# Windowed attention and a low-rank mixer on one core: head-pair scores on two 64-row halves, and batch 1's attention placed inside the first MLP chunk

## Chip, cores and metric

One core of a Trainium2 chip (trn2). The metric is the device time of one execution in microseconds (us), lower is better; 0.3% (1.2 us) is about what a measurement of this kernel can tell from no change.

## What is computed

Eight batches, eight heads, 576 positions, head size 64. Causal attention in a window of 64 positions, then, per batch, a mixer of rank 32 along the sequence and a two-layer MLP (512 to 2048 to 512), both with a residual:

```python
scores = scale * np.matmul(q, k.transpose(0, 1, 3, 2))
rel = pos[:, None] - pos[None, :]
scores = np.where((rel >= 0) & (rel < 64), scores, -1000000000.0)
attn = softmax(scores)
x = (attn @ v) with the heads side by side          # B, S, 512
u = x + ((x.transpose(0, 2, 1) @ U) @ V).transpose(0, 2, 1)
out = u + np.maximum(u @ w_ch1, 0.0) @ w_ch2
```

## The kernel before

All matmuls are in bf16. A batch has 576 = 9 blocks of 64 positions; a block of queries sees two blocks of keys. A tile named `un` holds 128 tokens of `u`, and the MLP works on nine chunks of 512 tokens across the batches, so chunk 0 needs batch 0 alone, chunk 1 batches 0 and 1, and so on.

**Attention of one batch** (`attention`) is a table of pieces. T: `TK`, `TQ` transpose keys and queries of a head pair on TensorE (L249 for batches 0 to 3, 12 transposes of 96 rows to 64 columns; L255 for the others) and copy them out of PSUM. Keys go by ScalarE into `kt` (L267). Queries go into a block-diagonal `qbd`, in which the other head's half is zero: one half by ScalarE (L276), the other by VectorE (L278), which waits for the first. S: `SC`, two per pair, computes the scores with 9 full matmuls per pair (L292, 128 keys by 128 columns, both heads at once), the exponential on ScalarE (L300), the mask on VectorE (L302). PV: five pieces of up to 16 matmuls (L320) that write the halves of PSUM's partitions by turns, then on VectorE a reciprocal (L329) and the normalisation into `xs` (L330). U, V: the mixer (L344, cast L352, L359) and on VectorE the sum with `xs` into `un` (L368). UT: transposes of `un` (L381) and copies into `uTc` (L385), which the MLP reads. Values of even blocks are needed shifted by 64 partitions: `shift_v` (L132 to 141) copies `vA` to `vB`.

**MLP of one chunk** (`mlp`) is 32 slots of four 512-column matmuls: slots 0 to 15 are the first layer (L407), evicted with relu by VectorE (odd, L416) and ScalarE (even, L418); slots 16 to 31 the second (L429), and after every fourth the residual sum into `osb` on VectorE (L438).

**Order.** The engines execute their instructions as the program writes them. Batch 0's attention comes first, alone. Then chunk 0's 32 slots, with nothing between, then batch 1's attention alone, with its value shifts on VectorE ahead of each PV. From chunk 1 on, `PLACE` says after which slot of chunk c a piece of batch c+1 is written (and T of batch c+2):

```python
PLACE = {"S": [0, 2, 4, 6, 8, 10, 12, 14], "PV": [16, 17, 18, 19, 20],
         "T": [16, 17, 18, 19, 20, 21, 22, 23], "U": [22], "V": [24, 25, 26],
         "UT": [26, 27, 28, 29, 30]}
```

Batch 2's T and S stand in chunk 1 too, from slot 4 (T) and 7 (S). PSUM: `ps_mm` has three one-bank buffers (MLP; three of four transposes of batches 0 and 1), `ps_big` two two-bank buffers (scores, PV, mixer), `ps_tp` one bank (all other transposes). Loads stand on GpSimd's queue.

Of the kernel before, what the change touches and what calls it, by code (L numbers as in the profile page):

```python
# [17 lines left out]
def kernel(  # L18
# [41 lines left out]
    pt_pool = ctx.enter_context(tc.tile_pool(name="pt", bufs=1))  # L60
# [13 lines left out]
    maskA = const.tile([P, 5, 2, W], BF16, name="maskA")  # L74
# [12 lines left out]
    qbd = [const.tile([P, 2, S], BF16, name=f"qbd{j}") for j in range(HP)]  # L87
# [75 lines left out]
    for i in range(2):  # L163
# [3 lines left out]
        out=maskA[:, 0, :, :],  # L167
        in_=maskA[:, 0, :, :],
# [7 lines left out]
        out=maskA[:, 1:5, :, :],  # L176
        in_=maskA[:, 1:5, :, :],
# [3 lines left out]
        pattern=[[0, 4], [0, 2], [-1, W]],  # L181
# [3 lines left out]
        out=maskA[:, 1:5, :, :],  # L185
        in_=maskA[:, 1:5, :, :],
# [3 lines left out]
        pattern=[[0, 4], [0, 2], [1, W]],  # L190
# [36 lines left out]
    def attention(b, spare=False):  # L227
# [6 lines left out]
        pts = [None] * HP  # L234
# [35 lines left out]
        def TQ(j):  # L270
            def f():
                tp = tr(qb, j)
                for g in range(2):
                    rs = slice(g * W, g * W + W)
                    if g == 0:
                        nc.scalar.copy(out=like(qbd[j][rs, g, :]), in_=tp[rs])  # L276
                    else:
                        nc.vector.tensor_copy(out=like(qbd[j][rs, g, :]), in_=tp[rs])  # L278
            return f

        def SC(j, part):
            blks = range(0, 5) if part == 0 else range(5, NB)
            n = len(blks)

            def f():
                if part == 0:
                    pts[j] = pt_pool.tile([P, NB, 2, W], BF16, name=f"pt{j}")
                pt = pts[j]
                sc = ps_big.tile([P, 2 * CH], FP32, name="sc", tag="big")
                for kk, blk in enumerate(blks):  # L290
                    w0 = 0 if blk == 0 else W * (blk - 1)
                    nc.tensor.matmul(  # L292
                        sc[:, kk * P : (kk + 1) * P],
                        kt[j][:, w0 : w0 + P],
                        qbd[j][:, :, blk * W : (blk + 1) * W],
                        start=True,
                        stop=True,
                    )
# [4 lines left out]
            return f

        def PV(t):
            def f():
# [4 lines left out]
                for h in range(H):  # L311
                    for blk in blks:
# [5 lines left out]
                        else:  # L318
# [3 lines left out]
                            pts[h // 2][:, blk, h % 2, :],  # L322
# [66 lines left out]
        pcs["S"] = [SC(j, a) for j in range(HP) for a in range(2)]  # L389
# [9 lines left out]
    def mlp(c):  # L399
# [68 lines left out]
    def values_and_mixing(b, a):
        for t in range(NT):
            if t < NFULL:  # L470
                shift_v(b, nc.vector, [t])
            a["PV"][t]()
        for part in ("U", "V", "UT"):
            for f in a[part]:
                f()


    att = {0: attention(0, True)}
    transposes_and_scores(att[0])
# [8 lines left out]
    for c in range(NCH):  # L488
        slots = [[] for _ in range(NSLOT)]

        def place(b, part):
            for f, s in zip(att[b][part], PLACE[part]):
                slots[s].append(f)

        if c == 0:
            att[1] = attention(1, True)
            for f in mlp(0):
                f()
            transposes_and_scores(att[1])
            for _ in load_kq(3, False):  # L500
                pass
            values_and_mixing(1, att[1])
            continue
        b = c + 1
        if b < B:
            shift_v(b, nc.gpsimd)
            if b + 1 < B:
                load_v(b + 1)
            if b + 2 < B:
                for _ in load_kq(b + 2, False):  # L510
                    pass
            if b == 2:
                att[2] = attention(2)
                for n, f in enumerate(att[2]["T"]):
                    slots[FIRST_T + n].append(f)
                for n, f in enumerate(att[2]["S"]):
                    slots[FIRST_T + 3 + n].append(f)
            else:
                place(b, "S")
            place(b, "PV")  # L520
            if b + 1 < B:
                att[b + 1] = attention(b + 1)
                place(b + 1, "T")
            for part in ("U", "V", "UT"):
                place(b, part)
        for fill, extra in zip(mlp(c), slots):
            fill()
            for f in extra:
                f()
# [30 lines left out]
```

## Time and profile before

| | |
|---|---|
| three runs | 389.4, 389.86, 390.8 us; median 389.86 |
| profiled execution | 390.55 us, of it 388.5 from first to last instruction |
| TensorE busy | 343.6 us (88%), 2739 matmuls |
| VectorE, ScalarE, GpSimd busy | 189.9, 144.7, 104.6 us |
| mean granted TensorE clock | 0.969 |
| chain that ended last | TensorE 78%, VectorE 9%, ScalarE 4%, GpSimd 3% |

Busy time overlaps between engines. The chain runs back from the last instruction, at each step to what released it. TensorE's matmuls are pipelined, so the distance of two starts tells the pace, not the length of a row. A granted clock of 1.0 is 2.4 GHz, 0.5 is 1.2 GHz; before its first recorded change it reads 1.0 whatever it was.

### The profile page before, as it was taken

The numbers are of one execution on the slowest core, as the hardware profiler recorded it, in microseconds if no ns is written. First come the engines' busy times: TensorE is split into PE (matmuls) and PEld (weight loads), VectorE is DVE, ScalarE is ACT, GpSimd is POOL, SyncE is SP. The second block draws the span as 40 slices with busy tenths as digits, with TensorE's granted clock in tenths as the row PEclk, the third lists the DMA queues.
The fourth block names the chain that finished last, engine by engine and source line by source line (L and its number), as shares of the span: only waits on it lengthen the run. The fifth ranks groups of instructions, "written<-read, shape, count | busy, mean of one in ns | idle before, by whom it ended". The sixth has DMA issues, their size and how long they took to land.

```text
span 388.5 us, 6618 instructions
## 1 busy us (share of the span) xinstructions
PE 343.6 (88%) x2739; PEld 179.6 (46%) x2784; DVE 189.9 (49%) x363; ACT 144.7 (37%) x245; POOL 104.6 (27%) x123
## 2 busy tenths in 40 slices
PE   4635999535999899999999999999999999999996
PEld 3522444422455455545554555455545545444442
DVE  6573231673267545654565357535753565322321
ACT  4603310903474335434543453355334503310300
POOL 8761243039302840168035702500000000000000
PEclk9999999955899999999999999999999999999999
DMA  7999999149404990299059904610001001002002
GB/s 101 136 205 200 185 170 204 46 28 126 31 2 29 133 132 2 13 122 158 1 35 111 148 0 43 76 54 2 30 27 57 0 29 56 27 27 80 3 27 84
DMA packets 91134, 28.52 MB, mean 73 GB/s; under 512 B 77152, under 2 KB 85472, under 8 KB 91104
## 3 DMA queue, kind: packets, MB, share of 16 engines
q0 software_dynamic: 84704, 18.50, 56.0%
q1 hardware_dynamic: 6400, 9.59, 7.1%
q8 instruction: 22, 0.36, 0.4%
q14 instruction: 8, 0.07, 0.1%
HBM read 37.14 MB, written 9.44 MB: 120 GB/s over the span
## 4 chain that ended last, share of the span: by engine, by line
PE 78%; DVE 9%; ACT 4%; POOL 3%; issue 2%; DMA 1%; another core or an unknown queue 1%; ACTq 0%; POOLq 0%
PE psA L407 32%; PE psU L429 30%; PE sc L292 3%; PE xr L320 3%; PE tpu L381 3%; PE tpn L255 3%; PE psv L359 2%; PE tpg L249 2%; DVE xs_99 L330 1%; DVE xs_100 L330 1%; ACT uTc L385 1%; DVE osb L438 1%; DMA vrep<-in_moe_V_dram 1%; PE pshh L344 1%; ACT qbd_115 L276 1%
## 5 line engine op out<-in xcount | busy, mean ns | idle before, releaser
L407 PE MATMUL psA<-uTc,w1b 128*128 128x512 bf16 x559 | 136.4, 387 | 1.6 <-ACT uTc L385 0.7
L407 PEld LDWEIGHTS <-w1b 128*128 128x128 bf16 x576 | 55.1, 100 | 59.1 <-issue 5.4
L438 DVE TENSOR_TENSOR osb<-psU,un 128x512 f32<-128x512 f32 x36 | 24.9, 691 | 70.8 <-PE psU L429 70.7
L385 ACT COPY uTc<-tpu 128x512 bf16<-128x512 bf16 x36 | 21.1, 585 | 42.8 <-PE tpu L381 42.8
L123 POOL DMA_DIRECT2D vA_102<-in_v_dram x16 | 14.1, 883 | 64.9 <-PE tpn L255 40.5
L123 POOL DMA_DIRECT2D vA_101<-in_v_dram x16 | 14.1, 882 | 45.0 <-PE tpg L249 22.5
L381 PE MATMUL tpu<-ident,un 128*128 128x128 bf16 x144 | 15.8, 240 | 4.7 <-ACT uTc L385 4.7
L381 PEld LDWEIGHTS <-un 128*128 128x128 bf16 x144 | 12.2, 108 | 13.8 <-issue 7.4
L359 PE MATMUL psv<-hh,vrep 128*128 128x512 bf16 x38 | 13.9, 428 | 3.0 <-ACT hh L352 1.3
L352 ACT CAST hh<-pshh 128x512 bf16<-128x512 f32 x8 | 4.7, 589 | 30.3 <-PE pshh L344 30.3
L368 DVE TENSOR_TENSOR un<-psv,xs_100 128x512 bf16<-128x512 f32 (+1 forms) x20 | 12.7, 685 | 3.3 <-PE psv L359 3.0
L330 DVE TENSOR_TENSOR xs_100<-xr,rcp 128x512 bf16<-128x512 f32 (+1 forms) x20 | 13.8, 692 | 0.7
L330 DVE TENSOR_TENSOR xs_99<-xr,rcp 128x512 bf16<-128x512 f32 (+1 forms) x20 | 13.8, 690 | 0.7
L368 DVE TENSOR_TENSOR un<-psv,xs_99 128x512 bf16<-128x512 f32 (+1 forms) x20 | 12.5, 682 | 2.6 <-remote 2.4
L329 DVE RECIPROCAL rcp<-xr 128x8 f32<-128x8 f32 (+1 forms) x40 | 8.2, 205 | 10.3 <-PE xr L320 9.1
L249 PE MATMUL tpg<-ident,kg 96*64 96x96 bf16 x144 | 5.8, 220 | 7.4 <-DMA kg<-in_k_dram 4.7
L249 PEld LDWEIGHTS <-kg 96*64 96x64 bf16 x192 | 6.4, 122 | 12.4 <-DMA kg<-in_k_dram 7.0
L267 ACT COPY kt_109<-tpg 128x576 bf16<-128x576 bf16 x4 | 2.5, 637 | 19.4 <-PE tpg L249 19.4
L114 POOL DMA_DIRECT2D kn_106<-in_k_dram x10 | 8.7, 871 | 2.6 <-PE tpn L255 2.6
L114 POOL DMA_DIRECT2D kn_105<-in_k_dram x10 | 8.8, 884 | 1.7 <-PE tpn L255 1.7
L114 POOL DMA_DIRECT2D qn_107<-in_q_dram x10 | 8.9, 892 | 0.9 <-PE tpn L255 0.9
L114 POOL DMA_DIRECT2D qn_108<-in_q_dram x10 | 8.8, 877 | 0.9 <-PE tpn L255 0.9
(700 smaller groups left out, 736.7 us busy)
## 6 DMA issues: line engine op xcount, KB each, us to landing
out_dram<-osb SPq DMA_DIRECT2D x36, 256.0 KB, 2.1
vA_101<-in_v_dram POOLq DMA_DIRECT2D x16, 128.0 KB, 5.4
w1b<-in_moe_w_ch_dram POOLq DMA_DIRECT2D x2, 1024.0 KB, 9.6
w2b<-in_moe_w_ch_dram POOLq DMA_DIRECT2D x2, 1024.0 KB, 17.8
vA_102<-in_v_dram POOLq DMA_DIRECT2D x16, 128.0 KB, 5.1
kg<-in_k_dram POOLq DMA_DIRECT2D x3, 576.0 KB, 13.7
qg<-in_q_dram POOLq DMA_DIRECT2D x3, 576.0 KB, 15.7
kn_105<-in_k_dram POOLq DMA_DIRECT2D x8, 128.0 KB, 4.5
```

Source lines behind the costliest of these rows:

```text
L114: nc.gpsimd.dma_start(out=dst[0:rows, t, :, :], in_=src[b, :, t * P : t * P + rows, :].rearrange("h p d -> p h d"),)
L123: nc.gpsimd.dma_start(out=va[:, t, :, 0:D], in_=v[b, :, t * P : (t + 1) * P, :].rearrange("h p d -> p h d"),)
L249: nc.tensor.transpose(tp[g * D : (g + 1) * D, c, :], src[:, 2 * j + g, c, :], ident[0:GP, 0:GP])
L255: nc.tensor.transpose(tp[:, t, :], src[:, t, 2 * j : 2 * j + 2, :].rearrange("p h d -> p (h d)"), ident[:],)
L330: nc.vector.tensor_tensor(out=x[lo:hi, t, :, :].rearrange("p (a h) d -> p a h d", a=2), in0=xv[:, :, :, 0:D], in1=rcp[lo:hi].to_broadcast( ...
L359: nc.tensor.matmul(ps[:, n, :], vrep[:, off : off + P], hh["sb"][:], start=True, stop=True)
L368: nc.vector.tensor_tensor(out=u_tiles[g][lo:hi, :], in0=ps[lo:hi, n, :], in1=x[lo:hi, t, :, :].rearrange("p h d -> p (h d)"), op=ALU.add,)
L381: nc.tensor.transpose(tp[:, dc, :], u_tiles[g][:, dc * P : (dc + 1) * P], ident[:])
L385: nc.scalar.copy(out=uT_of(g // TPC)[:, :, col : col + P], in_=tp[:])
L407: nc.tensor.matmul(ps[:], w1b[:, dc, i * P : (i + 1) * P], uTc[:, dc, :], start=(dc == 0), stop=(dc == NDC - 1),)
L429: nc.tensor.matmul(acc[t][:], c1[i][:, t * P : (t + 1) * P], w2b[:, i, :], start=(i == 0), stop=(i == NFC - 1),)
L438: nc.vector.tensor_tensor(out=osb[:], in0=acc[t][:], in1=u_tiles[g][:], op=ALU.add)
```

## The change

Scores: `qbd` goes; `TQ` copies both heads' queries at once into `qt` on VectorE. Each block's score becomes two matmuls of 64 rows and 64 columns, one per head, on rows 0 to 63 and 64 to 127 of the array and into the two banks of one `ps_big` buffer. Eight of the nine blocks of a pair share one exponential and one mask of 2 x 512; the ninth blocks of all four pairs share one (`SC8`). So S has 5 pieces, not 8, and 72 matmuls per batch, not 36.

Order: all pieces of batches 2 to 7 but T move two slots or more earlier; batch 2's T and S start at slots 0 and 3. Batch 1's T, S and first two PV go into the second layer of chunk 0; PV 2 to 4, U, V and UT stand behind its last slot.

Batches 0 and 1 (`alone`): the mixer's residual is a second matmul with the identity, and `un` is copied out by VectorE and ScalarE in turn. Batch 0's shifts are on ScalarE, batch 1's on GpSimd.

```diff
         def TQ(j):
             def f():
-                tp = tr(qb, j)
-                for g in range(2):
...
-                        nc.scalar.copy(out=like(qbd[j][rs, g, :]), in_=tp[rs])
...
-                        nc.vector.tensor_copy(out=like(qbd[j][rs, g, :]), in_=tp[rs])
+                nc.vector.tensor_copy(out=like(qt[j][:]), in_=tr(qb, j))
...
+        def scores(sc, n, j, blk):
+            w0 = 0 if blk == 0 else W * (blk - 1)
+            for g in range(2):
+                rs = slice(g * D, g * D + D)
+                nc.tensor.matmul(
+                    sc[:, g, n * W : (n + 1) * W],
+                    kt[j][rs, w0 : w0 + P],
+                    qt[j][rs, blk * W : (blk + 1) * W],
+                    start=True,
+                    stop=True,
+                )
+        def SC(j):
+            def f():
+                sc = ps_big.tile([P, 2, CH], FP32, name="sc", tag="big")
+                for blk in range(NB - 1):
+                    scores(sc, blk, j, blk)
+                dst = pts[:, j, :, 0 : NB - 1, :].rearrange("p g n w -> p g (n w)")
+                nc.scalar.activation(out=dst, in_=sc[:], func=ACT.Exp, scale=scale)
...
+        def SC8():
+            sc = ps_big.tile([P, 2, CH], FP32, name="sc8", tag="big")
+            for j in range(HP):
+                scores(sc, j, j, NB - 1)
...
+                    if alone:
+                        nc.tensor.matmul(
+                            ps[:, n, :],
+                            ident[:],
+                            x[:, t, :, :].rearrange("p h d -> p (h d)"),
+                            start=False,
+                            stop=True,
+                        )
...
+                    if alone:
+                        copy = nc.scalar.copy if n else nc.vector.tensor_copy
+                        copy(out=u_tiles[g][lo:hi, :], in_=ps[lo:hi, n, :])
+                        continue
...
-        "S": [0, 2, 4, 6, 8, 10, 12, 14],
-        "PV": [16, 17, 18, 19, 20],
+        "S": [1, 4, 7, 10, 12],
+        "PV": [14, 15, 16, 17, 18],
         "T": [16, 17, 18, 19, 20, 21, 22, 23],
-        "U": [22],
-        "V": [24, 25, 26],
-        "UT": [26, 27, 28, 29, 30],
+        "U": [20],
+        "V": [22, 23, 24],
+        "UT": [24, 25, 26, 27, 28],
...
+    PLACE_1 = {
+        "T": [22, 23, 24, 25, 26, 27, 28, 28],
+        "S": [24, 26, 28, 29, 29],
+        "PV": [30, 31, 32, 32, 32],
...
+    PLACE_2["T"] = [0, 1, 2, 3, 4, 5, 6, 7]
+    PLACE_2["S"] = [3, 5, 7, 9, 10]
...
+    shift_v(0, nc.scalar.copy, range(NFULL))
```

VectorE around the first PV pieces of batch 0, before; L139 and L141 are the value shifts, `xs` the normalised output:

```order
L483 CAST ub_97<-uf_95 128x160
L139 COPY vB_103<-vA_101 64x8x64
L329 RECIPROCAL rcp<-xr 128x8
L330 TENSOR_TENSOR xs_99<-xr,rcp 128x512
L139 COPY vB_103<-vA_101 64x8x64
L141 COPY vB_103<-vA_101 64x8x64
L329 RECIPROCAL rcp<-xr 128x8
```

ScalarE at the same place, changed (VectorE there keeps reciprocal and normalisation, by turns):

```order
L290 ACTIVATE pts<-sc 128x2x512 x2
L302 ACTIVATE pts<-sc_361 128x8x64
L141 COPY vB_100<-vA_98 64x8x64
L140 COPY vB_100<-vA_98 64x8x64
L141 COPY vB_100<-vA_98 64x8x64
```

The seven shifts left VectorE for ScalarE, where they stand behind the last exponential.

VectorE from chunk 0's last slots on, changed; the line numbers are the changed kernel's (L455 the sum into `osb`, L268 the query copy, L291 and L304 masks):

```order
L268 COPY qt_111<-tpg 128x576
L291 TENSOR_TENSOR pts<-pts,maskA 128x2x512
L455 TENSOR_TENSOR osb<-psU,un 128x512
L268 COPY qt_112<-tpg 128x576
L268 COPY qt_113<-tpg 128x576
L291 TENSOR_TENSOR pts<-pts,maskA 128x2x512 x2
L304 TENSOR_TENSOR pts<-pts,maskA 128x8x64
L330 RECIPROCAL rcp<-xr 64x8
L331 TENSOR_TENSOR xs_97<-xr,rcp 64x512
L455 TENSOR_TENSOR osb<-psU,un 128x512
```

Before, the four `osb` of chunk 0 stood together and all of batch 1 behind them; now query copies and masks stand between.

VectorE in chunk 2, slots 19 to 24, changed (L385 the sum into `un`):

```order
L455 TENSOR_TENSOR osb<-psU,un 128x512
L268 COPY qt_111<-tpn 128x576
L268 COPY qt_112<-tpn 128x576
L385 TENSOR_TENSOR un<-psv,xs_97 64x512
L385 TENSOR_TENSOR un<-psv,xs_97 128x512
L455 TENSOR_TENSOR osb<-psU,un 128x512
L268 COPY qt_113<-tpn 128x576
L385 TENSOR_TENSOR un<-psv,xs_97 128x512 x3
```

The last query copy now stands behind two sums into `un`; before, the last query copy stood ahead of all of them.

## Rows read from the trace of the kernel before

**Rows 1.** Busy time by stage: start:end, length, busy us (instructions) per engine, granted clock, DMA.

```profile
0.00:37.91 37.91, 18.74 (x230) 12.87 (x232) 22.21 (x59) 14.06 (x22) 22.69 (x37) 1.00 1.21 159
37.91:67.59 29.68, 29.58 (x126) 12.90 (x127) 7.60 (x11) 4.78 (x8) 10.64 (x11) 1.00 1.78 186
67.59:97.11 29.52, 15.09 (x235) 10.44 (x236) 16.86 (x35) 11.83 (x21) 12.78 (x16) 0.64 0.86 69
97.11:143.03 45.92, 42.55 (x448) 21.98 (x454) 24.63 (x42) 22.59 (x38) 19.07 (x19) 0.97 0.76 63
...
181.05:218.84 37.79, 36.93 (x297) 19.68 (x302) 20.62 (x39) 17.02 (x29) 15.70 (x18) 1.00 0.81 74
```

**Rows 2.** The same view, 2 us of batch 1's attention alone.

```profile
76.00:78.00 2.00, 1.60 (x18) 1.32 (x19) 1.31 (x4) 1.29 (x3) 0.00 (x0) 0.52 0.03 8
```

**Rows 3.** TensorE timeline, chunk 3: start, us, line, tile, shape, count.

```profile
181.75 0.44 PE L292 MATMUL sc<-qbd_113,kt_109 128*128 128x128 bf16 x5
182.02 1.89 PE L407 MATMUL psA<-uTc,w1b 128*128 128x512 bf16 x8
183.75 0.39 PE L292 MATMUL sc<-qbd_113,kt_109 128*128 128x128 bf16 x4
```

**Rows 4.** The same timeline around one PV piece (16 matmuls stand between the rows).

```profile
198.98 0.38 PE L429 MATMUL psU<-w2b,c_7_2288 128*128 128x512 bf16 x1
...
199.67 0.45 PE L255 MATMUL tpn<-ident,qn_108 128*128 128x128 bf16 x5
```

**Rows 5.** TensorE weight loads in chunk 3 by form: busy us, mean ns, idle before.

```profile
L320 PEld LDWEIGHTS <-pt_2209 128*64 128x64 bf16 x18 | 0.7, 108 | 2.1 <-issue 1.7 <-ACT kt_109 L267 0.4
L292 PEld LDWEIGHTS <-kt_111 128*128 128x128 bf16 x9 | 0.7, 98 | 0.5
```

**Rows 6.** TensorE timeline, one transpose piece of batch 2.

```profile
107.54 0.45 PE L249 MATMUL tpg<-ident,qg 96*64 96x96 bf16 x12
107.92 0.45 PE L292 MATMUL sc<-qbd_113,kt_109 128*128 128x128 bf16 x5
```

**Rows 7.** ScalarE and VectorE groups by form: busy us, mean ns, idle before.

```profile
L267 ACT COPY kt_109<-tpg 128x576 bf16<-128x576 bf16 x4 | 2.5, 637 | 19.4 <-PE tpg L249 19.4
L300 ACT ACTIVATE pt_1187<-sc 128x640 bf16<-128x640 f32 x1 | 0.7, 697 | 0.0
L300 ACT ACTIVATE pt_1187<-sc 128x512 bf16<-128x512 f32 x1 | 0.6, 603 | 0.0
L330 DVE TENSOR_TENSOR xs_99<-xr,rcp 128x512 bf16<-128x512 f32 x16 | 11.1, 691 | 0.6
L329 DVE RECIPROCAL rcp<-xr 128x8 f32<-128x8 f32 x32 | 6.6, 205 | 9.9 <-PE xr L320 9.1
L278 DVE COPY qbd_113<-tpg 64x576 bf16<-64x576 bf16 x2 | 1.5, 760 | 0.4 <-ACT qbd_113 L276 0.4
L302 DVE TENSOR_TENSOR pt_2209<-pt_2209,maskA 128x640 bf16<-128x640 bf16 x1 | 0.5, 493 | 1.5 <-ACT pt_2209 L300 1.5
```

**Rows 8.** TensorE's idle time: the transposes in chunk 1 (by form); waits in chunks 2 to 5 (us, times, longest).

```profile
L249 PE MATMUL tpg<-ident,kg 96*64 96x96 bf16 x96 | 3.6, 208 | 2.6 <-DVE qbd_115 L278 1.0 <-DVE qbd_113 L278 0.8 <-DVE qbd_114 L278 0.8
...
PE tpn L255 <- DVE qbd_115 L278: 1.6, 4, 0.4
```

**Rows 9.** VectorE timeline of batch 0: the last masks, the last normalisation.

```profile
17.72 0.91 DVE L302 TENSOR_TENSOR pt_347<-pt_347,maskA 128x640 bf16<-128x640 bf16 x2 [0.75 <-ACT pt_347 L300]
...
28.06 0.68 DVE L330 TENSOR_TENSOR xs_99<-xr,rcp 64x512 bf16<-64x512 f32 x1
```

**Rows 10.** ScalarE timeline of batch 1 alone: the mixer's cast, one `uTc` copy.

```profile
87.91 0.58 ACT L352 CAST hh<-pshh 128x512 bf16<-128x512 f32 x1 [10.09 <-PE pshh L344]
...
93.38 0.58 ACT L385 COPY uTc<-tpu 128x512 bf16<-128x512 bf16 x1 [0.67 <-PE tpu L381]
```

**Rows 11.** Batch 1's query load on GpSimd's queue; issue to landing of all query loads.

```profile
21.85 0.78 POOL L105 DMA_DIRECT2D qg<-in_q_dram  x1
...
DMA to landing us min/median/max: 3.4/5.8/24.9
```

More of the change, by code (lines that the diff above doesn't have):

```diff
@@ L86 @@
     kt = [const.tile([P, S], BF16, name=f"kt{j}") for j in range(HP)]
-    qbd = [const.tile([P, 2, S], BF16, name=f"qbd{j}") for j in range(HP)]
+    qt = [const.tile([P, S], BF16, name=f"qt{j}") for j in range(HP)]
+    pts = const.tile([P, HP, 2, NB, W], BF16, name="pts")
     loaded = {}
@@ L166 @@
     nc.gpsimd.affine_select(
[L167 to L168 removed]
+        out=maskA[:, :, 0, :],
+        in_=maskA[:, :, 0, :],
         compare_op=ALU.is_ge,
@@ L388, in attention @@
         pcs["T"] = [f for j in range(HP) for f in (TK(j), TQ(j))]
-        pcs["S"] = [SC(j, a) for j in range(HP) for a in range(2)]
+        pcs["S"] = [SC(j) for j in range(HP)] + [SC8]
         pcs["PV"] = [PV(t) for t in range(NT)]
@@ L468, in values_and_mixing @@
[L468 to L479, printed above, removed]
+        "U": [20],
+        "V": [22, 23, 24],
+        "UT": [24, 25, 26, 27, 28],
+    }
+    PLACE_1 = {
+        "T": [22, 23, 24, 25, 26, 27, 28, 28],
+        "S": [24, 26, 28, 29, 29],
+        "PV": [30, 31, 32, 32, 32],
+        "U": [32],
+        "V": [32, 32, 32],
+        "UT": [32, 32, 32, 32, 32],
+    }
@@ L480 @@
+    PLACE_2 = dict(PLACE)
+    PLACE_2["T"] = [0, 1, 2, 3, 4, 5, 6, 7]
+    PLACE_2["S"] = [3, 5, 7, 9, 10]
+    att = {0: attention(0, spare=True, alone=True)}
+    a = att[0]
+    for j in range(HP):
+        a["T"][2 * j]()
+        a["T"][2 * j + 1]()
+        if j > 0:
+            a["S"][j - 1]()
+    a["S"][HP - 1]()
+    a["S"][HP]()
     for _ in load_kq(2, False):
         pass
+    shift_v(0, nc.scalar.copy, range(NFULL))
+    for f in a["PV"]:
+        f()
     for i in range(2):
         nc.vector.tensor_copy(out=ub[i][:], in_=uf[i][:])
-    values_and_mixing(0, att[0])
+    for part in ("U", "V", "UT"):
+        for f in a[part]:
+            f()
@@ L485 @@
     load_v(2)
     for c in range(NCH):
[L489 to L503, printed above, removed]
+        slots = [[] for _ in range(NSLOT + 1)]
@@ L504, with place @@
+        def place(b, parts, where):
+            if b not in att:
+                att[b] = attention(b, alone=(b == 1))
+            for part in parts:
+                for f, s in zip(att[b][part], where[part]):
+                    slots[s].append(f)
         b = c + 1
         if b < B:
-            shift_v(b, nc.gpsimd)
-            if b + 1 < B:
+            shift_v(b, nc.gpsimd.tensor_copy)
+            if 3 <= b + 1 < B:
                 load_v(b + 1)
-            if b + 2 < B:
+            if 4 <= b + 2 < B:
@@ L524 @@
-            for part in ("U", "V", "UT"):
-                place(b, part)
-        for fill, extra in zip(mlp(c), slots):
+            where = {1: PLACE_1, 2: PLACE_2}.get(b, PLACE)
+            if b <= 2:
+                place(b, ("T",), where)
+            place(b, ("S", "PV"), where)
+            if 3 <= b + 1 < B:
+                place(b + 1, ("T",), PLACE)
+            place(b, ("U", "V", "UT"), where)
+            if b == 1:
+                slots[NSLOT - 4].append(lambda: [None for _ in load_kq(3, False)])
@@ L527 @@
+        for fill, extra in zip(mlp(c) + [lambda: None], slots):
             fill()
```

92 lines of the change are left out of this document (27 added, 65 removed).

## Prediction

> **What bounds the kernel now.** I read the table by stage first. In the steady chunks TensorE is busy for 36.93 of 37.79 us [rows 1]: there the matmuls themselves set the time, and an edit counts only by what it does on TensorE. Two stages differ. Batch 0 alone takes 37.91 us with TensorE busy for half of it, and batch 1 alone 29.52 us, of which TensorE is busy 15.09, at a mean granted clock of 0.64 [rows 1]. The reader should see that VectorE and ScalarE are not full there either (16.86 and 11.83): it is a chain of short steps that wait for each other. In that stage the granted clock reads 0.52 from 76 us on, 1.2 in place of 2.4 GHz [rows 2], some 8 us after the dense matmuls of chunk 0 ended at 67.59. The timelines then give the prices of single steps: a step is worth the distance of the starts on either side of it, since matmuls overlap.
>
> **Score matmuls.** Now: five take 182.02 - 181.75 = 0.27 us, 54 ns each [rows 3], with no gap at either end. 36 per batch make 1.96 us. Changed: 72 matmuls of 64 rows, 64 columns, with 128 columns of weights each, and five visits in which TensorE changes between whole array and halves. No row shows row halves. The nearest is PV, which uses the two column halves by turns: from the start of the last 512-column matmul before it to the first transpose behind it 0.69 us pass [rows 4]. A 512-column matmul takes 0.216 us of that (eight from 182.02 to 183.75 [rows 3]; a slot of four 0.866), so 16 matmuls of 65 columns with entry and exit cost 0.474. The 12 transposes, which use column halves too, need 0.38 us from their start to the next kind of work [rows 6]. 65 columns at 2.4 GHz are 27 ns; 16 in sequence would be 0.43 us and leave nothing for entry and exit, while in pairs they are 0.22 to 0.27. So halves run together, at about 16.5 ns each, and a visit costs about 0.2 beside them. The unknown is whether the weight load allows that for row halves, whose weights are 128 columns wide, not 64. A load of 128 columns shows 98 ns, one of 64 columns 108 [rows 5]: the wider is not the longer one. I therefore take 16.5 ns: 72 x 0.0165 + 5 x 0.2 = 2.2 us, **+0.24 us per batch**. The bounds: 13 ns (two halves of 64 columns at 2.4 GHz, nothing added) gives 0; 54 ns (each half like a whole score matmul now) gives 4.9 us, +2.9 per batch. Of the lower end I see no gain beyond that, since the visits are new.
>
> The Trainium skill speaks against this part of the change: TensorE: Matmul & The Clock Gate, section "LDWEIGHTS (loading the stationary operand)", says that a load's time goes with its columns alone, and that fewer rows make it no shorter. By that, and if two halves' loads take turns, 72 loads cost twice what 36 do, which is the third rival below, 400.1 us where the sum by the rows is 381.2; its figure of 107 ns for 128 columns does not fit the 54 ns at which whole matmuls with such loads follow each other here.
>
> **Batch 0 alone (37.91 us): -1.8.** The masks end at 18.63 and the last normalisation at 28.74 [rows 9], because VectorE does five times reciprocal and normalisation (0.205 + 0.691 [rows 7]) and seven value shifts by turns with TensorE. Now the shifts are on ScalarE behind the last exponential; I put the end of that at 18.5, 0.3 later than now, as an exponential of 1024 is about 1.0 us (0.603 for 512, 0.697 for 640) and a short ninth one follows. Seven copies at 0.63 (the nearest row, a copy of 576 columns, is 0.637 [rows 7]) end at 22.9; the last two normalisations then end near 24.6, and the casts of U, moved behind them, near 25.1, against 28.7: -3.6. Given back: five identity matmuls at half clock, 0.43 each, two eviction pairs at both engines, about +1.4 on this chain, and the larger masks on GpSimd ahead of the last query loads, up to +0.7, of which I count +0.4. Bounds -4 (the mixer's copies in parallel hide the added matmuls) and +1 (ScalarE's shifts are twice as long).
>
> **Chunk 0 and batch 1 (29.68 + 29.52 = 59.2 us): -7.2.** Slots 0 to 21 stay: 22 x 0.866 + 2.0 of cold start (29.68 less 32 x 0.866) = 21.1. Slots 22 to 31: 8.7 of MLP; eight transpose pieces at 0.38 + 0.095 for the entry = 3.8 [rows 6]; five score pieces 2.2; PV 0 about 0.3; and waits. The two transposes of a pair share one PSUM bank, so each waits for the copy before it (0.64 on ScalarE, 0.76 on VectorE [rows 7]), and VectorE has masks (0.49 for 640 columns [rows 7], so 0.7 for 1024) and `osb` in the same queue. Followed slot by slot this is hidden by the 0.866 of MLP in most slots and shows where a mask stands ahead of a query copy (about 0.3 and 0.6), in slot 28, where two pieces stand (1.2), and ahead of PV 0, which needs the last mask (0.9): 3.0. Sum 18.0. Behind the last slot: `osb` 0.7, normalisations 1 to 4 at 0.9 and the mixer's matmuls 0.7 until its cast starts: 5.0; the cast 0.6; from there to the first matmul of chunk 1 now 97.11 - 88.49 = 8.6 [rows 1, 10], of it five copies of `uTc` at 1.25 apart (0.58 + 0.67 idle [rows 10]); I take 7.3, as the clock should fall some 8 us after slot 31, so the mixer still runs at 2.4 GHz, and the evictions go in pairs. 21.1 + 18.0 + 12.9 = 52.0. Batch 1's queries are there by 21.85 + 0.78 + 24.9 = 47.5 at the latest [rows 11], slot 22 comes at about 57, so no load is waited for. Bounds: -11 (no waits, clock stays up) and -2 (the fourth case).
>
> **Chunk 1 (45.92 us): -0.5.** Its transposes wait 2.6 us [rows 8], because a query copy holds the bank for ScalarE's half and then VectorE's (0.63 + 0.76). One VectorE copy halves that: -1.3. Against it batch 2's transposes now stand in slots 0 to 7, while the clock is still at 1.2 GHz: +0.5. Scores +0.24. Bounds -2 and +2.
>
> **Chunks 2 to 6: +0.8.** Scores 5 x 0.24 = +1.2. The wait of the last key transpose, 0.4 in each of four chunks [rows 8], goes: -1.6. What is late next: the last query copy now stands on VectorE behind two sums into `un`, and the first UT needs its bank, about 0.3 in four chunks: +1.2. PV one slot earlier shares VectorE with two relus; VectorE is busy 20.6 of 37.8 us [rows 1], so that is covered. The shorter ScalarE work, the dropped memsets and the earlier end of UT are worth nothing: TensorE hides them.
>
> **Sum.** -1.8 - 7.2 - 0.5 + 0.8 = -8.7 against the profiled execution's 390.55 (388.5 of span), 381.85. That execution lies 0.7 above the median of the runs, so I name **381.2 us** against 389.86.
>
> **Rivals.**
> 1. *The halves take turns.* Then a half costs about 28 ns (64 columns at 2.4 GHz in sequence, 27 ns). Seven batches' scores stand between MLP matmuls, 7 x 72 = 504 halves, so each ns more costs 0.5 us: +5.8, **387.0**. For it: no row shows row halves together. Against it: the column halves of [rows 4].
> 2. *The waits eat the overlap.* If every transpose in chunk 0 waits for a copy that itself stands behind a mask or `osb`, each of eight loses 0.6 to 0.7 more: +5, **386.2**. For it: the 2.6 us of [rows 8] are such waits. Against it: 0.866 us of MLP between two pieces.
> 3. *The weight load sets the pace, and the kernel is slower.* If each half costs 54 ns, like a whole score matmul, +0.5 x 37.5 = +18.9, **400.1**. The place is TensorE between two MLP groups in chunks 0 to 6; it decides from 34 ns per half on, where 17.4 ns x 0.5 eat the 8.7. Against it: PV's loads at 16.5 ns each and the equal lengths of [rows 5]. For it: those loads are of 64 columns and 128 rows, the new ones of 128 and 64.
> 4. *The change does not do what it says* in batch 1's case: its chain would not shorten behind slot 31, where PV 2 to 4, the mixer and UT still stand alone. Then the term ends at its -2: **386.4**. For it: the chain of [rows 10] is untouched by the overlap; against it: the pieces that moved are most of the ones ahead of it.
>
> **How the numbers follow.** The forecast 0.55, halves in turn 0.2, waits 0.1, loads 0.1, the chain unshortened 0.05. The forecast's own range, from the terms' bounds not all at one end at once, is 375.5 to 386. The range of 8 in 10 reaches on over the first two rivals, **375.5 to 389**, and leaves out the third and the tails. Faster by over 0.3% (below 388.7; 0.3% is what a measurement of this kernel can tell): nearly all of the forecast's cases (0.53), six tenths of the first rival's (0.12), eight tenths of the second's and fourth's (0.12), 0.77. Within 0.3%: 0.07. Slower: 0.16, the third rival and the upper tails.
>
> **What would show it.** The distance from a score piece's start to the next MLP matmul in a steady chunk: 0.37 us (16 matmuls and the exit) by the forecast, 0.55 by the first rival, 0.96 by the third. The first MLP matmul of chunk 0 near 36 us, of chunk 1 near 88 (now 97.11). Chunk 3 of 37.5 to 38.2 us (now 37.79). The transposes' wait in chunk 1 near 1.3 (now 2.6). The forecast is wrong if chunk 3 exceeds 39, or if chunk 0 and batch 1 take over 57.

## The result: 377.89 us against 389.63, inside the range, with the gain in other places than forecast

Four runs of the changed kernel took 375.09 to 379.35 us, median **377.89**; four of the kernel before 387.75 to 390.8, median 389.63. The ratio is 0.9695, 95% interval 0.9625 to 0.9764. The profiled execution of the change is the slowest of its four (379.35, span 377.3), so stages below are set against spans of 388.5 before and 377.3 after: 11.2 us.

The profile page after: busy time, and the chain that ended last.

```profile
PE 343.0 (91%) x3030; PEld 170.1 (45%) x3082; DVE 177.5 (47%) x313; ACT 131.1 (35%) x200; POOL 108.6 (29%) x125
...
PE 84%; DVE 5%; ACT 5%; issue 2%; POOL 2%; DMA 1%; ACTq 0%; DVEq 0%; POOLq 0%
```

TensorE is as busy as before (343.6 us), so nearly all of the gain is idle time taken out of its queue. Busy time by stage, in the columns of [rows 1]: batch 0 alone, chunk 0 with batch 1, chunk 1, chunk 3.

```profile
0.00:34.64 34.64, 17.78 (x271) 11.98 (x273) 16.15 (x39) 16.51 (x24) 22.67 (x36) 0.97 1.19 157
34.64:90.23 55.59, 45.36 (x397) 21.79 (x403) 21.08 (x34) 15.72 (x24) 27.85 (x30) 0.87 1.46 149
90.23:134.06 43.83, 42.44 (x483) 20.91 (x491) 23.48 (x39) 17.42 (x27) 18.62 (x19) 0.96 0.77 65
171.46:208.64 37.18, 36.77 (x334) 18.43 (x338) 20.14 (x36) 14.52 (x22) 15.71 (x18) 1.00 0.83 77
```

[rows 1] cuts the stages of the kernel before up to 0.2 us behind the first MLP matmul (at 97.11 for 96.91, for instance). From first matmul to first matmul its chunk 0 with batch 1 is:

```profile
37.91:96.91 59.00, 44.47 (x360) 23.19 (x363) 24.46 (x46) 16.61 (x29) 23.22 (x27) 0.82 1.32 128
```

All stages by their first matmuls:

| stage | before | after | measured | forecast |
|---|---|---|---|---|
| batch 0 alone | 37.91 | 34.64 | -3.3 | -1.8 |
| chunk 0 and batch 1 | 59.00 | 55.59 | -3.4 | -7.2 |
| chunk 1 | 45.96 | 43.83 | -2.1 | -0.5 |
| chunk 3 (of 2 to 6) | 37.80 | 37.18 | -0.6 | +0.2 |

Chunks 2 to 6 give -2.4 together where +0.8 was forecast. The stage that was to bring most brought about half of it, and three others made up for it.

**The score matmuls.** TensorE timeline of chunk 3, two score pieces, to set beside [rows 3]:

```profile
173.29 0.41 PE L275 MATMUL sc<-qt_110,kt_106 64*128 64x64 bf16 x16
173.62 2.76 PE L424 MATMUL psA<-uTc,w1b 128*128 128x512 bf16 x11
176.32 0.41 PE L275 MATMUL sc<-qt_111,kt_107 64*128 64x64 bf16 x16
```

From a piece's start to the next MLP matmul 0.33 us pass (forecast 0.37). With the way in, the five visits of chunk 3 cost 2.06 us, against 2.00 for the eight visits before.

**The waits in chunk 0 and batch 1.** What TensorE waited for there (us in total, times, longest), the largest lines:

```profile
PE tpu L398 <- ACT uTc L402: 3.0, 4, 1.0
PE tpg L245 <- DVE qt_112 L268: 1.9, 1, 1.9
PE xr L321 <- DVE xs_97 L331: 1.4, 2, 1.0
...
PE tpg L245 <- ACT kt_109 L263: 0.8, 1, 0.8
```

The one long wait, 1.9 us, comes from a mask on VectorE that took 1.54 us while GpSimd shifted batch 2's values. VectorE, then GpSimd:

```profile
62.05 0.69 DVE L291 TENSOR_TENSOR pts<-pts,maskA 128x1024 bf16<-128x1024 bf16 x1 [2.19 <-ACT pts L290]
...
65.60 1.54 DVE L291 TENSOR_TENSOR pts<-pts,maskA 128x1024 bf16<-128x1024 bf16 x1 [2.19 <-ACT pts L290]
```

```profile
63.18 1.89 POOL L135 COPY vB_100<-vA_98 64x2048 bf16<-64x2048 bf16 x1 [5.42 <-DMA vA_98<-in_v_dram]
65.13 1.47 POOL L136 COPY vB_100<-vA_98 64x1536 bf16<-64x1536 bf16 x1
```

Behind that mask stood `osb` and the query copy that the next transposes needed. TensorE then ran thin, and the clock fell with MLP slots still to come (2 us stretches; the granted clock is the number before the last two):

```profile
66.00:68.00 2.00, 0.56 (x3) 0.17 (x2) 2.00 (x3) 0.00 (x0) 0.60 (x1) 1.00 0.68 109
68.00:70.00 2.00, 0.76 (x24) 0.63 (x23) 0.40 (x1) 0.64 (x1) 0.00 (x0) 1.00 0.48 151
70.00:72.00 2.00, 1.67 (x26) 0.76 (x20) 1.12 (x2) 1.02 (x1) 0.00 (x0) 0.56 0.00 0
72.00:74.00 2.00, 2.00 (x29) 1.04 (x28) 0.33 (x1) 1.05 (x2) 0.00 (x0) 0.58 0.00 0
...
82.00:84.00 2.00, 2.00 (x5) 0.76 (x5) 0.69 (x1) 0.18 (x1) 2.00 (x4) 0.52 2.24 130
```

It fell again for the mixer, at 80 to 84 us. Before, it had fallen after chunk 0's dense matmuls [rows 2].

### The profile page after: what moved, and what is told of

Read it like the earlier page. It is cut to its first block, busy times and chain, and to the rows that moved or that the text cites. A ratio compares the mean times of both kernels' runs of the same rounds, so it can differ in the third digit from the quotient of the medians.

```text
span 377.3 us, 7086 instructions
## 1 busy us (share of the span) xinstructions
PE 343.0 (91%) x3030; PEld 170.1 (45%) x3082; DVE 177.5 (47%) x313; ACT 131.1 (35%) x200; POOL 108.6 (29%) x125
## 4 chain that ended last, share of the span: by engine, by line
PE 84%; DVE 5%; ACT 5%; issue 2%; POOL 2%; DMA 1%; ACTq 0%; DVEq 0%; POOLq 0%
PE psA L424 35%; PE psU L446 31%; PE xr L321 3%; PE tpn L251 3%; PE psv L360 3%; PE sc L275 3%; PE tpu L398 3%; PE tpg L245 2%; ACT pts L290 1%; PE pshh L345 1%; ACT uTc L402 1%; DMA qg<-in_q_dram 1%; DVE xs_97 L331 1%; DVE osb L455 1%; PE psv L368 1%
## 5 line engine op out<-in xcount | busy, mean ns | idle before, releaser
L424 PE MATMUL psA<-uTc,w1b 128*128 128x512 bf16 x556 | 135.0, 388 | 2.0 <-ACT uTc L402 0.7
L424 PEld LDWEIGHTS <-w1b 128*128 128x128 bf16 x576 | 53.9, 99 | 63.3 <-issue 5.2
L455 DVE TENSOR_TENSOR osb<-psU,un 128x512 f32<-128x512 f32 x36 | 24.8, 690 | 59.5 <-PE psU L446 56.5
L291 DVE TENSOR_TENSOR pts<-pts,maskA 128x1024 bf16<-128x1024 bf16 x32 | 23.0, 719 | 36.3 <-ACT pts L290 36.3
L290 ACT ACTIVATE pts<-sc 128x1024 bf16<-128x1024 f32 x32 | 32.7, 1022 | 14.7 <-PE sc L275 14.7
L402 ACT COPY uTc<-tpu 128x512 bf16<-128x512 bf16 x36 | 21.1, 586 | 32.3 <-PE tpu L398 32.3
L321 PEld LDWEIGHTS <-pts 128*64 128x64 bf16 x576 | 14.7, 115 | 18.7 <-issue 11.7
L398 PE MATMUL tpu<-ident,un 128*128 128x128 bf16 x144 | 14.7, 228 | 5.6 <-ACT uTc L402 5.6
L245 PE MATMUL tpg<-ident,kg 96*64 96x96 bf16 x168 | 7.0, 224 | 8.0 <-DMA kg<-in_k_dram 5.2
L385 DVE TENSOR_TENSOR un<-psv,xs_97 128x512 bf16<-128x512 f32 (+1 forms) x15 | 9.8, 687 | 5.2 <-PE psv L360 5.2
L385 DVE TENSOR_TENSOR un<-psv,xs_96 128x512 bf16<-128x512 f32 (+1 forms) x15 | 9.5, 683 | 3.4 <-PE psv L360 3.4
L321 PE MATMUL xr<-vA_99,pts 128*64 128x65 bf16 x160 | 8.9, 197 | 1.6 <-DVE xs_97 L331 1.4
L114 POOL DMA_DIRECT2D kn_103<-in_k_dram x10 | 8.7, 872 | 4.9 <-PE tpn L251 4.9
```

The source lines that it names most:

```text
L245: nc.tensor.transpose(tp[g * D : (g + 1) * D, c, :], src[:, 2 * j + g, c, :], ident[0:GP, 0:GP])
L290: nc.scalar.activation(out=dst, in_=sc[:], func=ACT.Exp, scale=scale)
L291: nc.vector.tensor_tensor(out=dst, in0=dst, in1=maskA.rearrange("p g n w -> p g (n w)"), op=ALU.mult)
L321: nc.tensor.matmul(xr[r0 : r0 + W, h // 4, (h % 4) * VW : (h % 4 + 1) * VW], pts[:, h // 2, h % 2, blk, :], rhs, start=True, stop=True,)
L398: nc.tensor.transpose(tp[:, dc, :], u_tiles[g][:, dc * P : (dc + 1) * P], ident[:])
L402: nc.scalar.copy(out=uT_of(g // TPC)[:, :, col : col + P], in_=tp[:])
```

## Experiments

All ratios are to the kernel before, measured on the same chip. Stage lengths are from profiled executions, from first MLP matmul to first MLP matmul.

### 1. Whole-array scores in the new order

```diff
-   sc[:, g, ...]  <- kt[j][rows of g], qt[j][rows of g]      # 2 x 64 rows
+   sc[:, a, ...]  <- kt[j][:, ...], qbd[j][:, :, blk]         # 128 rows, block-diagonal
-   nc.vector.tensor_copy(qt[j], tp)
+   nc.scalar.copy(qbd[j] upper half, tp); nc.vector.tensor_copy(qbd[j] lower half, tp)
```

> The changed kernel with the old score matmuls (whole array, block-diagonal queries, two copies per query tile), eight blocks per piece and the ninth apart, in the new order. Theory (the row halves run in pairs and a visit has no entry cost, so a batch's scores fell from 1.96 to 1.58 us): a score piece of eight matmuls takes 0.43 us, the ninth blocks 0.22, chunk 3 grows from 37.18 to 37.6 plus up to 0.4 for the transpose wait that the second query copy brings back, so 37.6 to 38.0; the whole is 3 to 6 us over 377.3. Rival (the steady gain of 0.6 per chunk comes from the new order alone): chunk 3 stays within 0.1 of 37.18 and the whole within 1 us.

386.1 us (385.35 to 389.63), ratio 0.9948 (0.9887 to 1.0009): most of the gain is gone, and the interval includes no gain at all. Chunk 3 took 38.20 us, but the scores are not why: their five visits cost 2.01 us, as with halves. The waits in chunks 2 to 5, where the change shows none on its transposes:

```profile
PE tpn L254 <- DVE qbd L273: 3.3, 8, 0.4
```

That is 0.8 of the 1.0 us per chunk. In chunk 1 the transposes wait 2.4 us again, and the stage takes 46.10 us, as before. **The halves are not faster than whole matmuls; what they buy is a query layout that one copy fills**, so that the transposes' bank comes free in time.

### 2. Eight halves on one side, then eight on the other

```diff
-   for blk in range(8): for g in (0, 1): scores(sc, blk, j, blk, g)
+   for g in (0, 1): for blk in range(8): scores(sc, blk, j, blk, g)
```

> The changed kernel with each score piece's matmuls in another order: all eight of the upper half, then all eight of the lower. Theory (the 0.34 us piece comes from two halves at work at once, which needs them by turns): at 27 ns each in sequence the piece takes 0.50 us or more, chunk 3 grows by 4 x 0.16 + 0.1 = 0.75 to 37.9 or more. Rival (a 64-column matmul simply costs 17 ns wherever it stands): the piece stays at 0.34 and chunk 3 at 37.2.

382.66 us (380.82, 384.51), ratio 0.983 (0.970 to 0.996); chunk 3 37.70. A piece's start to the next MLP matmul is now 0.47 us instead of 0.33:

```profile
176.31 0.54 PE L275 MATMUL sc<-qt,kt 64*128 64x64 bf16 x16
176.78 2.76 PE L426 MATMUL psA<-uTc,w1b 128*128 128x512 bf16 x11
```

So alternate halves do overlap: 8 to 9 ns each are saved, 0.5 us per chunk where I had said 0.75 or more. The single starts behind these merged lines show how. In the change the two halves of a pair start 3 ns apart, and one pair 29 ns after the other; in run 2 neighbours on the same half start 29 ns apart, which is the first rival's 28 ns, and the lower half begins while the last three matmuls of the upper one are still to come.

### 3. Batch 2's shift behind the next value loads

```diff
-   shift_v(2) on GpSimd, then load_v(3)
+   load_v(3), then shift_v(2) on GpSimd
```

> The changed kernel with batch 2's value shift on GpSimd written behind batch 3's value loads, so that it runs after chunk 0. Theory (that shift, 63.2 to 66.6 us, holds VectorE's mask up, 1.54 us for 0.69, and the mask the query copy, and so TensorE waits 1.9 us and its clock falls at 70 us): the mask takes 0.7, the wait of the sixth transpose piece falls from 1.9 to about 1.0, the clock stays at 2.4 GHz up to slot 31, chunk 0 with batch 1 goes from 55.8 to 53 or less. Rival (the wait is the queue order of VectorE alone): waits within 0.3 of now, chunk 0 with batch 1 over 55.

376.83 us (375.06, 378.59), ratio 0.968 (0.9555 to 0.9805). No GpSimd copy runs at that mask any more, and it is short again:

```profile
65.86 0.69 DVE L291 TENSOR_TENSOR pts<-pts,maskA 128x1024 bf16<-128x1024 bf16 x1 [2.19 <-ACT pts L290]
```

The transposes' longest wait fell from 1.9 to 1.0 us, so 0.9 us of it is shown to come from the copy on GpSimd; the other 1.0 stays, with the mask and `osb` still ahead of the query copy. The stage took 54.27 us and the clock still read 0.60 and 0.55 from 70 to 74: the fall needs no collision. Nor does 54.27 prove a gain: run 9 executes chunk 0 and batch 1 as the change does and took 54.04 there, so the same code varies by 1.5 us in this stage.

### 4. The residual sum on VectorE for batches 0 and 1

```diff
-   att = {0: attention(0, spare=True, alone=True)} ... attention(b, alone=(b == 1))
+   att = {0: attention(0, spare=True)} ... attention(b)
```

> The changed kernel with the residual of batches 0 and 1 as a VectorE sum again, no identity matmuls and no copies by ScalarE. Theory (at 1.2 GHz the added matmuls cost more than the copies in parallel save): from the end of the mixer's cast to the first matmul of the next chunk 8.87 falls to about 7.9 (batch 0) and 9.3 to about 8.6 (batch 1), 1 to 2 us less in all. Rival (the split of the evictions pays): 1 us or more slower.

375.69 us (375.39, 376.0), ratio 0.9651 (0.9585 to 0.9717). The two stages:

```profile
0.00:33.01 33.01, 17.03 (x266) 11.74 (x268) 16.89 (x41) 15.44 (x22) 22.72 (x36) 1.00 1.16 145
33.01:86.11 53.10, 43.50 (x393) 21.19 (x399) 21.44 (x36) 14.64 (x22) 27.21 (x29) 0.88 1.56 166
```

Batch 0 is 1.6 us shorter. Of this 1.0 is shown to be the identity matmuls and the copies by turns: from the cast of `hh` to chunk 0's first matmul it is 9.47 us with them and 8.49 without, and ScalarE's first copy into `uTc` starts 5.5 instead of 4.1 us after that cast, because ScalarE evicts `un` first; the cast itself came 0.65 earlier, for which the edit gives no reason, and in run 8, with the same edit, it came at 25.22 us as in the change (25.17) and batch 0 took 33.72. At batch 1 cast to first matmul fell from 9.67 to 9.01; the rest of that stage's 2.5 lies within its scatter, or in the collision with the GpSimd copy, which this order all but misses (the mask took 0.77 us).

### 5. Batch 0's shifts on VectorE

```diff
-   shift_v(0, nc.scalar.copy, range(NFULL)); for f in a["PV"]: f()
+   for t in range(NT): shift_v(0, nc.vector.tensor_copy, [t]) if t < NFULL; a["PV"][t]()
```

> Batch 0's value shifts on VectorE again, one or two ahead of each PV piece as in the kernel before; all else as changed. Theory (ScalarE's copies are what took batch 0's gain): the last normalisation moves from 23.9 us back to 27 to 28.5, the first MLP matmul from 34.6 to 37.5 to 39, the time to 380.5 to 382.5 us; with the mixer's identity matmuls that is later than the kernel before (37.9) or level with it. Rival (the chain of batch 0 hangs on the loads and the masks, not on who shifts): first MLP matmul at most 35.6, the time at most 379.

381.31 us (377.99 to 381.82), ratio 0.9767 (0.971 to 0.9824). The first MLP matmul came at 36.93, 2.3 later: in between the two, nearer to the theory. The last normalisation ended at 26.18 instead of 23.89, the same 2.3 (the change, then this run):

```profile
23.21 0.68 DVE L331 TENSOR_TENSOR xs_96<-xr,rcp 64x512 bf16<-64x512 f32 x1
...
25.50 0.68 DVE L331 TENSOR_TENSOR xs<-xr,rcp 64x512 bf16<-64x512 f32 x1
```

VectorE's copies are shorter than ScalarE's (0.30 against 0.62), yet TensorE waits for them, because they stand between normalisations:

```profile
PE xr L321 <- DVE vB L140: 4.5, 3, 1.7
```

The kernel before ended at 28.74 [rows 9] with the same copies on VectorE. The change also turned round the two copies of a tile, so that the one PV needs comes first; VectorE idles at most 0.42 us per PV step in this run, 0.75 in the kernel before. And the first shift starts at 17.90 us here, at 18.97 before, behind masks that ended 0.8 us later and the casts of U. I had counted neither.

### 6. No overlap: batch 1 wholly behind chunk 0

```diff
+   if b == 1: slots[NSLOT] += T, S, PV, U, V, UT of batch 1, over the spare banks
```

> Batch 1's attention wholly behind chunk 0's MLP again, its transposes over the spare banks as in the kernel before; all else as changed. Theory (the overlap pays little, because half of batch 1's chain stays behind slot 31 and the pieces inside wait): chunk 0 and batch 1 together 56 to 58 us against 55.6, the time 378 to 380.5. Rival (the overlap brings the stage's whole gain and more): 59 us or more, the time from 381 on. By the term of the prediction (overlap and a higher clock together 7.2 us of 59.2) it would be the rival.

378.27 us (378.09 to 378.53), ratio 0.9714 (0.9682 to 0.9745): the same as the change. Chunk 0 and batch 1 took 54.28 us, chunk 1 44.30. **As the change places it, the overlap brings nothing that the medians show** (377.89 and 378.27). The change's executions scatter more, though: its fastest took 375.09 us, run 6's 378.09, and of that one there is no trace. The stretch from batch 1's first transposes to the mixer's cast, alone, and last the cast in the change:

```profile
64.58 0.45 PE L245 MATMUL tpg<-ident,kg 96*64 96x96 bf16 x12
...
70.95 0.82 PE L275 MATMUL sc<-qt,kt 64*128 64x64 bf16 x24 [1.46 <-DVE qt L268]
...
78.89 0.59 ACT L353 CAST hh<-pshh 128x512 bf16<-128x512 f32 x1 [5.78 <-PE pshh L345]
...
80.56 0.58 ACT L353 CAST hh<-pshh 128x512 bf16<-128x512 f32 x1 [6.10 <-PE pshh L345]
```

14.3 us from chunk 0's end to the cast. In the change slots 22 to 31 take 19.8 us, 11.1 over their MLP, and another 4.7 pass from there to the cast: 15.8. Over four banks T and S run alone in about 8 us; through one bank, between MLP slots, they take TensorE's own 6 us (8 x 0.475 and 2.06 at full clock) and the waits, at half clock in part. Of the pieces that leave TensorE idle longest, three PV, the mixer and UT stay outside.

### 7. Batch 1 ten slots earlier

```diff
-   "T": [22 .. 28, 28], "S": [24, 26, 28, 29, 29], "PV": [30, 31, 32, 32, 32], "U": [32], "V": [32, 32, 32], "UT": [32] * 5
+   "T": [12 .. 19], "S": [14, 16, 18, 20, 21], "PV": [23 .. 27], "U": [28], "V": [30, 31, 32], "UT": [31, 32, 32, 32, 32]
```

> Only batch 1's places in chunk 0 change: transposes in slots 12 to 19, scores in 14 to 21, PV in 23 to 27, U in 28, V in 30 to 32, UT in 31 and 32. Theory (what was left behind slot 31, and the two pieces in slot 28, cost the missing 3.8 us): chunk 0 and batch 1 together 46 to 49 us against 55.6, the granted clock at 1.0 up to slot 31, the time 369 to 372. Rival (the waits on copies behind masks and osb go along with the pieces, and the clock falls wherever attention and MLP mix): 53 us or more, the time from 375 on.

373.13 us (372.18 to 375.23), ratio 0.9588 (0.9549 to 0.9628). Chunk 0 and batch 1: 50.89, between the two expectations. The granted clock stayed at 1.0 up to 84 us, as the theory said; the waits on query copies came along, as the rival said: 2.2 us before transposes and 1.0 before scores. One of the three stands behind a mask that met batch 1's own value shift (1.35 us), the other two behind masks of 0.69 us and a relu or `osb` in VectorE's queue. Batch 2's shift met the last two masks, 2.25 and 1.68 us. With PV and the mixer inside, the overlap pays 3 to 5 us (against 54.0 to 55.6).

### 8. Runs 3, 4 and 7 together

> The earlier places, batch 2's value shift behind the next value loads, and the residual sum on VectorE for batches 0 and 1. Theory (the three parts act in different places): batch 0 alone 33.0 us as with the sum alone, chunk 0 and batch 1 another 1 us shorter than with the early places alone, since only the part of the identity matmuls that stands behind slot 31 still shows; the time 366.5 to 369.5 us. Rival (once the pieces lie under the MLP, the sum on VectorE stands in the way of osb and relus, as VectorE serves four kinds of steps there): no faster than the early places alone less the 1.6 us of batch 0.

368.09 us (367.62 to 371.63), ratio 0.9471 (0.9421 to 0.9522). Chunk 0 with batch 1, and chunk 1:

```profile
33.72:80.83 47.11, 41.98 (x398) 19.52 (x398) 21.65 (x36) 14.55 (x22) 22.96 (x24) 1.00 1.48 167
80.83:122.85 42.02, 41.73 (x494) 20.46 (x492) 23.92 (x39) 17.32 (x27) 23.46 (x25) 1.00 1.11 87
```

The time is as expected, its parts are not: batch 0 took 33.72 us and not 33.0, the first stage here 3.8 us less than in run 7 where I had said 1, and chunk 1 2.2 less (44.27 there), which ran at 1.00 instead of 0.94. No mask of batch 1 exceeds 0.88 us, against 2.25 in run 7.

### 9. The old places of PV, U, V and UT in the steady chunks

```diff
-   "PV": [14 .. 18], "U": [20], "V": [22, 23, 24], "UT": [24 .. 28]
+   "PV": [16 .. 20], "U": [22], "V": [24, 25, 26], "UT": [26 .. 30]
```

> In the steady chunks PV, U, V and UT stand in the slots of the kernel before (16 to 30) again, two later than in the change, beside the same transposes; row halves and the one query copy stay. Theory (the single query copy gives the steady gain of 0.6 us per chunk): chunk 3 at 37.1 to 37.35 us against 37.18. Rival (the new order of the pieces gives it): 37.6 to 37.85, as before. In time the two differ by some 2 us, 378 against 380.

377.24 us (374.94 to 378.98), ratio 0.9686 (0.9634 to 0.9738). Chunk 3:

```profile
169.48:206.61 37.13, 37.13 (x339) 18.45 (x338) 20.31 (x36) 14.52 (x22) 15.71 (x18) 1.00 0.84 77
```

The theory holds: the new order of these pieces gives nothing, the single query copy gives the 0.6 us. (S keeps its five new places, of which the first is not earlier, slot 1 for 0; run 1 has them too, at 38.20.) Since the other pieces stand as before, they can be set side by side: from the MLP matmul ahead of a piece to the one behind it, three places with key transposes fell from 1.69 to 1.13, 1.14 to 1.01 and 1.06 to 0.98 us. That is 0.8 us per chunk, twice the 0.4 that [rows 8] lists as waits.

### 10. Run 6 with batch 1's shifts on VectorE

```diff
-   shift_v(1, nc.gpsimd.tensor_copy) at the start of chunk 0
+   shift_v(1, nc.vector.tensor_copy, [t]) ahead of each PV of batch 1
```

> Batch 1 wholly behind chunk 0, and its value shifts on VectorE by turns with PV as in the kernel before. Theory (what shortened chunk 0 and batch 1 from 59.0 us is the shift that GpSimd makes inside chunk 0, not the overlap of the transposes and scores): chunk 0 and batch 1 at 57.3 to 59 us against 54.3 without this edit, the time 381 to 383. Rival (the shifts hide behind other steps of the chain, and the stage got shorter by the single query copies and by exp and mask of 1024): at most 55.3, the time at most 379.5.

380.13 us (379.45 to 380.75), ratio 0.9765 (0.9736 to 0.9793); the stage 56.74, 2.5 us more than in run 6, with 4.4 us of PV's waits on VectorE's shifts:

```profile
PE xr L321 <- DVE vB L140: 4.4, 3, 1.7
```

So GpSimd's shift is worth 2.5 of the 4.7 us by which run 6 beats the 59.00 before, less than the theory said. The other 2.2 should lie in the copies, exponentials and masks; that is not shown, as I did not take them apart.

### 11. The mixer and UT of batch 1 earlier still

```diff
-   "PV": [23 .. 27], "U": [28], "V": [30, 31, 32], "UT": [31, 32, 32, 32, 32]
+   "PV": [22 .. 26], "U": [27], "V": [28, 29, 31], "UT": [30, 31, 32, 32] and slot 9 of chunk 1
```

> The best version so far with batch 1's PV in slots 22 to 26, U in 27, V in 28, 29 and 31, UT in 30 to 32, and its last UT, whose columns chunk 2 alone reads, in slot 9 of chunk 1. Theory (five UT steps of 1.05 us each stand between chunk 0 and chunk 1): three of them lie under the MLP, chunk 0 and batch 1 at 44.3 to 46 us against 47.1, the time 365 to 367.3. Rival (UT waits there for V's sums, which stand behind osb and the normalisations on VectorE): 46.8 or more, the time 367.5 or more.

368.21 us (367.97 to 368.33), ratio 0.9458 (0.9434 to 0.9481), no faster than run 8; the stage 47.15. The rival was right: V's sums hold VectorE until 77 us, when the last MLP slot ends.

```profile
74.35 2.61 DVE L385 TENSOR_TENSOR un<-psv,xs 64x512 bf16<-64x512 f32 x4 [1.24 <-PE psv L360]
77.59 0.69 DVE L455 TENSOR_TENSOR osb<-psU,un 128x512 f32<-128x512 f32 x1 [0.63 <-PE psU L446]
```

### 12. Run 8 with two banks for the last transposes

```diff
-   tp = ps_tp.tile(..., name="tpu")
+   tp = a bank of ps_mm if b <= 1 and t % 2 else ps_tp.tile(..., name="tpu")
```

> The earlier places, late shift and sums on VectorE as before, and the last transposes of batches 0 and 1 (UT) by turns in the one bank for transposes and in a bank that the MLP leaves free there. Theory (the tail behind slot 31 and behind batch 0 is a chain of transposes 0.38 us and copy 0.6 us through one PSUM bank, 1.05 us a step): each step falls to the copy's 0.6 to 0.7 us, batch 0 alone from 33.7 to about 32.3 us, chunk 0 and batch 1 from 47.1 to about 45.7, the time 365 to 366.5 us against 368.1. Rival (the steps follow the sums of V on VectorE, 0.6 to 0.7 us each, or the copies' own hand-over): less than 0.5 us in each place, 367.3 or more.

**366.51 us** (365.49 to 367.89), ratio 0.9398 (0.9351 to 0.9445): the lowest median, though its interval overlaps run 8's a little. The steps fell as the theory says, to 0.6 us (but for one of 1.0 at batch 1, which waited for a sum of V), and chunk 0 began at 31.31. But chunk 0 and batch 1 took 49.36 us, 2.2 more than in run 8 and 3.7 more than expected: slot 12 now came before batch 1's keys and queries.

```profile
PE tpg L245 <- DMA kg<-in_k_dram: 2.3, 1, 2.3
PE tpg L245 <- DMA qg<-in_q_dram: 1.8, 1, 1.8
```

The second wait ended at 48.34 us, later than the 47.5 by which the prediction had all queries landed. Behind these waits the granted clock read 0.51 from 46 to 50 us. That the places should move some slots later in this version was not tried.

## Why the prediction was right in sum and wrong in its parts

- **Score matmuls (+0.24 per batch): right in kind, too high.** The five visits measured 2.06 us against my 2.2, and 2.00 before: +0.06. The step that held is that halves run together, taken from PV's column halves [rows 4]; run 2 shows it for row halves. The third rival fell: loads of 64 rows and 128 columns last 94 to 95 ns, hardly less than the 98 of whole ones [rows 5], and yet follow each other every 21 ns, exit included. For the same reason the 54 ns that the prediction holds against the length of a load decide nothing: they are a pace, and loads overlap.

```profile
L275 PEld LDWEIGHTS <-kt_107 64*128 64x128 bf16 x18 | 0.4, 95 | 0.4 <-issue 0.4
```

- **Batch 0 (-1.8): -3.3.** The shifts' 0.63 us each measured 0.62. The end of normalisation came at 23.89, not 24.6, and U began at 24.10, not 25.1: the shifts began at 17.57, 0.9 us earlier than I had put them, and the +0.4 for the larger masks did not show. Of the 4.9 us by which the normalisation ends earlier, ScalarE's shifts are 2.3 (run 5); the prediction gave them, with the moved casts, all of its 3.6. From the last normalisation to the first MLP matmul 10.75 us passed, 9.17 before: +1.6, near the +1.4 given back.
- **Chunk 0 and batch 1 (-7.2): -3.4.** The terms that failed are "slots 22 to 31: 18.0" and the "7.3" behind the cast. The slots took 19.8: the long mask was not foreseen, and between 70 and 74 us, in slots 29 and 30, the granted clock read 0.56 and 0.58. I had let the clock fall only some 8 us after slot 31, which ended at 75.8; it fell a second time at 80.5. So the mixer began at 1.2 GHz, with twice the matmuls: 9.1 us from the cast's end, not 7.3. In run 9, where the clock read 1.0 there, it was 7.4: that term failed by the clock alone. Slots 0 to 21 took 21.4 for 21.1. Beyond these sizes the premise failed: run 6 shows that the overlap, to which I credited the stage, is worth little or nothing here. What shortened the stage is GpSimd's shift (run 10) and, as far as is known, the shorter steps. The fourth rival, to which I gave 0.05, named this, but its price was too pessimistic.
- **Chunk 1 (-0.5): -2.1.** I let the single query copy halve the transposes' wait of 2.6 us [rows 8]. It took it away whole: two copies one after the other (0.63 and 0.76 [rows 7]) exceed the 0.866 us of MLP between two pieces, one of 0.75 does not. Run 1 brings back the second copy and the wait.
- **Chunks 2 to 6 (+0.8): -2.4.** The wait of the key transposes went, as said, and with it the places where they stand lost 0.8 us per chunk (run 9), not the 0.4 that I read from [rows 8]. The new wait that I charged for the first UT (+1.2) did not come: TensorE's waits in chunks 2 to 5 hold none on the transposes' bank.
- **Rivals.** Halves taking turns: 29 ns is what run 2 makes of them, not the change. Waits eating the overlap: the transposes' waits were 1.9, 0.8, 0.4 and 0.2 us, not eight of 0.65. Loads: no.

Against the profiled execution the sum missed by 2.5 us (381.85 and 379.35): errors of +3.8 in one stage and of -6.3 in the others partly cancelled. That the time came so near is partly luck; a total inside its range says little about the steps.

## What to carry to other kernels

A chain of short steps laid into a dense stretch saves at most the idle time it had alone and what a lower clock cost there, and only if the steps with most idle time go in and nothing in the queues stalls them; price the same chain without overlap first. A layout that removes one of two copies out of a shared PSUM bank can be worth more than the matmuls it was made for: compare the copies' sum with the distance between the pieces. And a step made earlier may meet a load that has not landed, as run 12 did.

## What the runs showed of the hardware that I had not expected

A mask on VectorE that meets a GpSimd copy waits for its end. The traces of the change and the experiments hold fifteen masks of 1024 columns that were lengthened so, to between 0.77 and 2.27 us, and each ended 0.54 or 0.55 us after the copy did, whenever it had begun; in the change 65.60 + 1.54 = 67.14 against 65.13 + 1.47 = 66.60. The reverse shows in run 7, where the second copy, 1.47 us elsewhere, begins under the mask and ends 1.33 us after it:

```profile
65.38 2.25 DVE L291 TENSOR_TENSOR pts<-pts,maskA 128x1024 bf16<-128x1024 bf16 x1 [1.55 <-ACT pts L290]
```

```profile
65.19 1.89 POOL L135 COPY vB<-vA 64x2048 bf16<-64x2048 bf16 x1 [5.24 <-DMA vA<-in_v_dram]
67.14 1.81 POOL L136 COPY vB<-vA 64x1536 bf16<-64x1536 bf16 x1
```

The Trainium skill (SBUF — State Buffer, section "SBUF: two separate sides") states that a VectorE instruction with two SBUF inputs and a GpSimd instruction that reads SBUF lock a common pair of ports for a whole instruction each, and do not share it. The traces agree: the mask, 0.69 us alone, has 0.54 to 0.55 of them still to do when the copy ends.

The same instructions in chunk 0 and batch 1 took 55.59 us in the change and 54.04 in run 9. The granted clock read about 0.5 for the mixer in the one (0.52 from 82 to 84) and 1.0 from 76 to 88 in the other: with thin stretches in a stage, when the clock falls is itself uncertain. Only runs 8 and 11 show 1.00 in that stage from the first recorded change, at 38.3 us, to its end.
